# Batch 0 of an FFT-mixing and gated-FFN kernel: slices of x folded as they land, another order of sums, products and weight preparation

## The chip, the cores and the metric

The kernel runs on one core of a Trainium2 chip. The core has a matrix engine (TensorE, PE in the profile; its weight loads are PEld), three engines for elementwise work (VectorE or DVE, ScalarE or ACT, GpSimd or POOL), a queue engine that issues most transfers (SyncE or SP), and 16 DMA engines. The metric is the device time in microseconds.

## The reference

```python
# x: (8, 3008, 256) float32; w_gate, w_val: (256, 1536); w_out: (1536, 256)
X = np.fft.fft(x, axis=1)
X = np.fft.fft(X, axis=2)
x = X.real.astype(np.float32).reshape(8 * 3008, 256)
gate = 1.0 / (1.0 + np.exp(-(x @ w_gate)))
val = x @ w_val
out = (gate * val @ w_out).astype(np.float32)
```

The three weights are float64, because a float32 array is multiplied there by a float64 scalar. The kernel is handed their bits and makes float32 of them itself.

## The kernel before, in words

The real part of the two-dimensional transform splits into sums over the sequence and sums over the 256 features. The feature sums are linear, so the kernel multiplies them into the weights once: a **merge** multiplies 256 columns of `w_gate` or `w_val` by a cosine and sine table (`dt`) and leaves them as `G1` (cosine part) and `G2` (sine part). Per batch there remain the sequence sums. x is **folded** first (rows s and S-s, s and M+s are added or subtracted, and features d and 256-d likewise), then multiplied by a cosine table (giving **P**) and a sine table (giving **Q**); the one feature without a partner, number 128, gives a single row **E**, the same for all features. The tables lie in `ST`: 126 rows, 6 slots q, 753 columns for each of cosine and sine. Each sum makes half of the rows in an even and an odd part (`ev`, `od`); `places` adds and subtracts these into `pk` (P) or `qk` (Q), two VectorE instructions a group (L504, L507) after a ScalarE copy of `ev` (L499).

The main loop then goes over 576 **steps** i: 8 batches, 6 chunks of 252 rows, 12 tiles of 128 hidden features. Three steps make a group p. A step does, in the order of the code:

- `front_a(i)`: two TensorE products of `G1` with P. In batch 0's first chunk, steps 0 to 4 (`N1 = 5`) also get E by two products of `G2` with `e0`, a tile of zeros with E in its first row.
- `part(i)`: ScalarE copies the bank, doubled, as `ae` (L611); in steps 5 to 11 VectorE adds E instead, by two instructions (L614).
- `gate_a(i-1)`: a sigmoid of the step before (ScalarE, L630), and the values of the mirrored rows, z (VectorE, L635 or L632).
- `seed(i+1)`: from step 12 on, ScalarE writes E times its weight `ge` into the next step's bank (two instructions, L595), so that the products are added to it.
- `gate_b(i-1)`: a product (L647), a sigmoid of z (L648), a second product (L649), which frees the bank; then 13 GpSimd sums per group (L653) for the last product.
- what is in `pre` and `use`: weight preparation; a part of `forms`, which makes sums of `w_out` blocks (GpSimd for g = 0, otherwise VectorE, and four ScalarE copies).
- `back`: from step 5, ten instructions a step of the output product, a block scheme with 15 products, in banks `po0` to `po4`.
- `front_b(i)`: two products of `G2` with Q, added to the same bank.
- `side`: x of later batches, tables, E rows of later chunks.

Five of the eight PSUM banks are the `po` banks. Three (`psx`) are shared by the steps' banks `pf`, merges (`ps`) without a bank of their own, and the sequence sums.

A weight (256 rows or columns of one matrix, 18 `jobs`) is loaded by `weight_load` (L288), taken apart by two ScalarE instructions (`weight_parts`, L295 and L296), put together by three VectorE instructions and one GpSimd addition (`weight_join`, L305, L306, L308, L310), and merged by `weight_use` (eight TensorE instructions, ScalarE copies L331 and L332, and two small transfers `ge` on SP, L334). Weights 0 to 9 (`KEEP = 10`) have places of their own, later ones use x's.

Every engine, SP too, works in the order in which the code issues instructions (`manual_schedule`). SP's start is: weights 0 and 1, x of batch 0 in two halves (L150), the cosine table in two halves (L192), weights 2 to 4, half the sine table, weights 5 and 6, the other half, weights 7 to 9. The sums of batch 0 wait for the folds of three slots at a time; P and E sums (24 wide matmuls, E as 128 equal rows) come before the Q sums (12). All TensorE instructions have line L134, that of the helper `mm`.

Of the kernel before, what the change touches and what calls it, by code (L numbers as in the profile page):

```python
# [81 lines left out]
def kernel(  # L82
# [61 lines left out]
    def load_x(b):  # L144
        X[b] = xp.tile([P, 4, NQ, D], F32, name="x4", tag="x4")
        for h in range(0, 4, 2):
            if b:
                nc.sync.dma_start(out=X[b][:, h : h + 2], in_=XR[b][:, h : h + 2])
            else:
                nc.sync.dma_start(out=X[b][0:NP, h : h + 2], in_=xf[b, :, h : h + 2])  # L150
# [29 lines left out]
    G1 = const.tile([P, 2, F], F32, name="G1")  # L180
    G2 = const.tile([P, 2, F], F32, name="G2")
# [8 lines left out]
    def load_table(t, nq):  # L190
        for q in range(0, NQ, nq):
            yield nc.sync.dma_start(out=ST[0][0:NP, t, q : q + nq], in_=stab[:, t, q : q + nq])  # L192
# [14 lines left out]
    def table_odd():  # L207
# [21 lines left out]
        def tangent():  # L229
# [8 lines left out]
    jobs = [(0, 0), (1, 0), (0, 1), (1, 1), (2, 0), (0, 2), (1, 2), (2, 1), (0, 3), (1, 3), (0, 4), (2, 2),  # L238
            (1, 4), (0, 5), (1, 5), (2, 3), (2, 4), (2, 5)]
    RAW, WS = {}, {}  # L240
    shared = {}
    KEEP = 10

    def weight_load(j):
# [13 lines left out]
        def home(j):  # L258

            if j in (0, 1, 2, 3, 5):  # L260
                if j > 2:
                    ws = some(5, pqp, "qk")[:, (j // 5) * 2 * WC : (j // 5 + 1) * 2 * WC]
                    return sp.tile([P, 4 * WC], F32, name="raw", tag="sf"), ws
                t = hp.tile([P, 6 * WC], F32, name="raw", tag="h")
                return t[:, 0 : 4 * WC], t[:, 4 * WC :]
            if j in (4, 6, 9):
                t = wf[:, {4: 1, 6: 2, 9: 3}[j]].rearrange("p m n -> p (m n)")
                return t[:, 0 : 4 * WC], t[:, 4 * WC : 6 * WC]
            t = some(10, cp, "c")
            if j == 7:  # L270
                raw = pqp.tile([P, 4 * WC], F32, name="raw", tag="pk")
                return raw, t[:, 6 * WC : 8 * WC]
            return t[:, 0 : 4 * WC], t[:, 4 * WC : 6 * WC]
# [50 lines left out]
    def merge(ws, g, c, other):  # L324
# [6 lines left out]
        nc.scalar.copy(G2[:, g, cs], ps[:, WC : 2 * WC])  # L331
        nc.scalar.copy(G1[:, g, cs], ps[:, 0:WC])  # L332
# [48 lines left out]
    def fold_ops(b, nq):  # L381
# [51 lines left out]
        else:  # L433

            def half1(q):
                point(nc.vector, 2, 3, q)
                first(nc.vector, 2, 3, q)
                for blk in range(2):
                    across(nc.vector, blk, q)
                    feat(nc.vector, *parts[blk], q)  # L440

            def half2(q):
                across(nc.vector, 0, q)
                feat(nc.vector, *parts[0], q)
                across(pool, 1, q)
                feat(pool, *parts[1], q)
            for q in qs:
                point(nc.vector, 0, 1, q)
            first(nc.vector, 0, 1, slice(0, NQ))
            point(pool, 2, 3, qs[1])  # L450
            first(pool, 2, 3, qs[1])
            ops += [lambda: half1(qs[0]), lambda: half2(qs[1])]
        for blk, (v, r) in enumerate(parts):
            if b and blk:
                W[b, blk] = v[:, :, HD:D], r[:, :, HD:D]
                continue
            W[b, blk] = (v[:, :, 0:HD], r[:, :, 0:HD],
                         v[:, :, HD : HD + 1].to_broadcast([v.shape[0], NQ, P]))
# [56 lines left out]
    def seq_start(b):  # L515
        PQE[b] = [pqp.tile([P, NK + 1], F32, name=name, tag=name) for name in ("pk", "qk")]
        if not b:
            PQE[b].append(op.tile([P, NK + 1], F32, name="ek", tag="os"))
# [5 lines left out]


# [60 lines left out]
    N1 = 5  # L586

    def seed(i):
# [5 lines left out]
        for g in range(2 if i >= NFT else 0):  # L594
            nc.scalar.activation(PF[i][:, g], EK[i // NFT], AF.Copy, scale=ge[:, g, f : f + 1])  # L595

    def front_a(i):
        (pk, *_), ks, _, _, fs = cut(i)
        if i < NFT:
            seed(i)  # L600
        for g in range(2):
            mm(PF[i][:, g], G1[:, g, fs], pk[:, ks], i < NFT and g == 0, True)
        for g in range(2 if i < N1 else 0):
            mm(PF[i][:, g], G2[:, g, fs], shared["qk"][:, 4 * WC : 4 * WC + CH], False, True)

    def part(i):
# [3 lines left out]
        if not N1 <= i < NFT:  # L610
            nc.scalar.activation(AP[i], PF[i], AF.Copy, scale=2.0)  # L611
            return
        for g in range(2):
            nc.vector.scalar_tensor_tensor(out=AP[i][:, g], in0=pqe[2][:, ks],  # L614
                                           scalar=ge[:, g, f : f + 1], in1=PF[i][:, g],
                                           op0=ALU.mult, op1=ALU.add)
# [6 lines left out]
    def gate_a(i):  # L623
# [7 lines left out]
        if N1 <= i < NFT:  # L631
            nc.vector.scalar_tensor_tensor(out=z[:, :, ::-1], in0=AP.pop(i), scalar=2.0, in1=PF[i],  # L632
                                           op0=ALU.mult, op1=ALU.subtract)
        else:
            nc.vector.tensor_tensor(z[:, :, ::-1], AP.pop(i), PF[i], op=ALU.subtract)  # L635
# [6 lines left out]
    def gate_b(i):  # L642
# [5 lines left out]
        nc.scalar.activation(pf[:, 0], z[:, 0], AF.Sigmoid)  # L648
        nc.vector.tensor_tensor(h[:, fh, n:], pf[:, 0], z[:, 1], op=ALU.mult)  # L649
# [94 lines left out]

    nc.gpsimd.memset(nil, 0.0)
# [3 lines left out]
    for j in range(2):  # L749
        weight_load(j)  # L750
    load_x(0)
    for _ in load_table(0, NQ // 2):
        pass
    for j in range(2, 5):
        weight_load(j)
    sines = load_table(1, NQ // 2)
    next(sines)
    for j in range(5, 7):
        weight_load(j)
    next(sines)  # L760
    for j in range(7, KEEP):
        weight_load(j)

    def weight_round(*js):
        for j in js:
            weight_parts(j)
            weight_join(j)

    weight_parts(0)
    weight_parts(1)  # L770
    weight_join(0)
    weight_join(1)
    weight_use(0)
    weight_use(1)
    seq_start(0)

    e0 = shared["qk"][:, 4 * WC : 4 * WC + CH]
    nc.gpsimd.memset(e0, 0.0)
    other = {(0, 0): (4, None), (0, 1): (4, None), (0, 2): (0, 1), (1, 2): (2, 3)}
    cos = [seq_group(0, blk, what, other.get((blk, what))) for blk in range(2) for what in (0, 2)]  # L780
    for i, f in enumerate(fold_ops(0, NQ // 2)):
        f()
        for sums, _, _ in cos:
            sums(*range(i * NQ // 2, (i + 1) * NQ // 2))
    sin = [seq_group(0, blk, 1, other.get((blk, 1))) for blk in range(2)]
    for i in range(2):
        for sums, _, _ in sin:
            sums(*range(i * NQ // 2, (i + 1) * NQ // 2))
    evacuate = [then for _, then, _ in cos + sin]
    for then, js in zip(evacuate, ((2, 3), (4,), (5,), (6,), (7,), (8,))):  # L790
        weight_round(*js)
        then()()
    nc.scalar.dma_start(out=ed[0:1], in_=PQE[0][2][0:1])
    nc.vector.tensor_copy(e0[0:1], PQE[0][2][0:1, 0:CH])
    weight_parts(9)
    for j in range(KEEP, KEEP + 3):
        weight_load(j)
    weight_use(2)
# [8 lines left out]
    pre, use = {}, {}  # L807
    for j, i in enumerate((0, 1, 2, 3, 4, 5, 6, 7, 9), 9):
        if i:
            pre.setdefault(i - 1, []).append(lambda j=j: weight_parts(j))  # L810
        pre.setdefault(i, []).insert(0, lambda j=j: weight_join(j))
        if KEEP <= j < len(jobs) - 3:
            at(i, lambda j=j: weight_load(j + 3))
    for j, i in enumerate((0, 0, 1, 2, 0, 3, 4, 5, 4, 6, 7, 8, 8, 8, 11), 3):
        use.setdefault(i, []).append(lambda j=j: weight_use(j))
# [123 lines left out]
```

## Time and profile before

| | |
|---|---|
| time, median of 3 runs | 1955.66 us (1949.49 to 1955.82) |
| profiled execution: span (no other time of it is given) | 1953.1 us |
| busy: PE, PEld | 1915.7 us (98%), 1788.2 us (92%) |
| busy: DVE, ACT, POOL | 1457.9 us (75%), 1332.5 us (68%), 1598.4 us (82%) |
| granted TensorE clock, mean | 0.995 |
| first Q product of step 0 starts at | 58.12 us |
| step 15 starts at | 122.31 us |

A row of the timeline gives start, duration, engine, line, operation, what is written and read, the number of instructions, and in brackets the idle time ahead of it with what ended it. A row of the windows gives the stretch, its length, the busy time (and count) of PE, PEld, DVE, ACT and POOL, the granted TensorE clock, the share of the DMA engines and GB/s. A TensorE matmul of 32-bit numbers shows as two instructions.

### The profile page before, as it was taken

Reading aid. Unit: us, or ns where it says so; the run is one execution under the profiler, and the core shown is the slowest. Engines: PE = TensorE matmul, PEld = TensorE weight load, DVE = VectorE, ACT = ScalarE, POOL = GpSimd, SP = SyncE. Lnnn points to the kernel's source line nnn. Section 1 sums busy time; section 2 is a strip of 40 time slices with the busy share of each in tenths; the row PEclk is TensorE's granted clock in tenths of the full one; section 3 lists DMA queues with packets and bytes.
Section 4 is the critical chain, followed back from the end, with each engine's and each line's share of the span. In section 5 each row is a group of like instructions: output and inputs, shape, how many; then the busy total and the mean of one; then the engine's idle time right before and its main releaser. Section 6 shows DMA issues by size and latency. Waiting matters only on the chain.

```text
span 1953.1 us, 34554 instructions
## 1 busy us (share of the span) xinstructions
PE 1915.7 (98%) x11252; PEld 1788.2 (92%) x11252; DVE 1457.9 (75%) x3271; ACT 1332.5 (68%) x3122; POOL 1598.4 (82%) x2853
## 2 busy tenths in 40 slices
PE   6999999999999999999999999999999999999997
PEld 3789889999999999999999999999999999999997
DVE  5877787787777877777777777777777777777776
ACT  2567757776777677776777767777677766777775
POOL 3679998997889788997889869888789886777776
PEclk8999999999999999999999999999999999999999
DMA  9352513112012020212012021111200110011011
GB/s 268 91 134 20 117 32 111 46 25 82 14 46 58 16 79 14 60 46 79 14 25 80 16 79 25 45 51 21 83 17 14 22 20 14 14 22 20 14 20 27
DMA packets 169746, 96.78 MB, mean 50 GB/s; under 512 B 133858, under 2 KB 161636, under 8 KB 167020
## 3 DMA queue, kind: packets, MB, share of 16 engines
q1 hardware_dynamic: 167610, 94.06, 20.2%
q8 instruction: 90, 1.47, 0.3%
q10 hardware_dynamic: 1926, 0.52, 0.1%
q14 instruction: 88, 0.72, 0.1%
q0 software_dynamic: 32, 0.00, 0.0%
HBM read 69.83 MB, written 46.71 MB: 60 GB/s over the span
## 4 chain that ended last, share of the span: by engine, by line
PE 92%; DVE 4%; DMA 2%; ACT 1%; issue 0%; SPq 0%; POOL 0%; DVEq 0%; ACTq 0%; POOLq 0%
PE pf L134 48%; PE po L134 40%; PE ev L134 3%; DMA st<-in_stab_dram 1%; DVE c L700 1%; PE od L134 1%; DMA ge<-G 1%; PE ps L134 1%; DVE z L635 0%; ACT pf L648 0%; DVE h L649 0%; DVE h L647 0%; DVE ae L614 0%; DVE wf L370 0%; DMA raw<-in_moe_w_gate_dram 0%
## 5 line engine op out<-in xcount | busy, mean ns | idle before, releaser
L653 POOL TENSOR_TENSOR sf<-h 128x168 f32<-128x168 f32 (+1 forms) x960 | 533.3, 575 | 222.3 <-DVE h L649 222.3
L653 POOL TENSOR_TENSOR sf<-h,sf 128x168 f32<-128x168 f32 (+1 forms) x1152 | 645.1, 580 | 63.0 <-DVE h L649 62.6
L134 PE MATMUL pf<-qk,G 128*128 128x252 f32 (+1 forms) x2304 | 583.1, 376 | 4.3 <-DVE ae L614 2.4
L134 PE MATMUL pf<-pk,G 128*128 128x252 f32 (+1 forms) x2304 | 583.2, 376 | 1.5 <-DVE h L649 1.5
L649 DVE TENSOR_TENSOR h<-pf,z 128x252 f32<-128x252 f32 (+1 forms) x576 | 241.7, 420 | 425.0 <-ACT pf L648 425.0
L595 ACT ACTIVATE pf<-ek,ge 128x252 f32<-128x252 f32 (+1 forms) x1128 | 531.6, 471 | 18.6 <-DVE h L649 0.2
L134 PE MATMUL po<-sf,wf 128*128 128x168 f32 (+1 forms) x3072 | 529.9, 305 | 0.0
L611 ACT ACTIVATE ae<-pf 128x504 f32<-128x504 f32 (+1 forms) x569 | 335.5, 590 | 233.3 <-PE pf L134 232.3
L134 PEld LDWEIGHTS pf<-pk,G 128*128 128x128 f32 x2304 | 436.1, 190 | 55.3 <-DVE h L649 2.6
L134 PEld LDWEIGHTS po<-sf,wf 128*128 128x128 f32 x3072 | 472.7, 190 | 8.2
L134 PE MATMUL po<-h,wf 128*128 128x168 f32 (+1 forms) x2688 | 476.0, 305 | 0.2 <-DVE wf L367 0.2
L700 DVE TENSOR_TENSOR c<-c 128x168 f32<-128x168 f32 (+1 forms) x949 | 447.7, 504 | 5.5 <-ACT c L677 0.2
L134 PEld LDWEIGHTS po<-h,wf 128*128 128x128 f32 x2688 | 427.5, 190 | 17.2 <-DVE wf L367 0.6
L134 PEld LDWEIGHTS pf<-qk,G 128*128 128x128 f32 x2304 | 409.8, 190 | 31.9 <-ACT ae L611 3.2
L635 DVE TENSOR_TENSOR z<-ae,pf 128x504 f32<-128x504 f32 (+1 forms) x569 | 378.7, 666 | 23.4 <-ACT h L630 21.8
L630 ACT ACTIVATE h<-pf 128x252 f32<-128x252 f32 (+1 forms) x576 | 218.1, 379 | 156.3 <-PE pf L134 151.9
L648 ACT ACTIVATE pf<-z 128x252 f32<-128x252 f32 (+1 forms) x576 | 214.4, 372 | 114.8 <-DVE h L647 112.2
L647 DVE TENSOR_TENSOR h<-h,pf 128x252 f32<-128x252 f32 (+1 forms) x576 | 232.7, 404 | 0.0
L653 POOL TENSOR_TENSOR sf<-sf 128x168 f32<-128x168 f32 (+1 forms) x192 | 111.0, 578 | 15.1
L653 POOL TENSOR_TENSOR sf<-sf,h 128x168 f32<-128x168 f32 (+1 forms) x192 | 105.2, 548 | 0.0
L677 ACT COPY c<-po 128x504 f32<-128x504 f32 (+1 forms) x144 | 81.9, 569 | 2.6 <-PE po L134 2.6
L134 PE MATMUL ev<-st,x 63*128 63x189 f32 (+3 forms) x372 | 73.6, 348 | 10.2 <-DVE x L398 7.9
(138 smaller groups left out, 874.9 us busy)
## 6 DMA issues: line engine op xcount, KB each, us to landing
x<-xr SPq DMA_DIRECT2D x14, 1536.0 KB
out_dram<-os SPq DMA_DIRECT2D x380, 56.0 KB
xr<-in_xf_dram SPq DMA_DIRECT2D x14, 768.0 KB
xr<-in_xf_dram SPq DMA_DIRECT2D x35, 256.0 KB
ek<-ed SPq DMA_DIRECT2D x39, 126.0 KB
out_dram<-os SPq DMA_DIRECT2D x288, 7.0 KB
st<-in_stab_dram SPq DMA_DIRECT2D x4, 1111.9 KB
x<-in_xf_dram SPq DMA_DIRECT2D x2, 1512.0 KB
```

The lines of the kernel that those rows point to most:

```text
L134: nc.tensor.matmul(o, l, r, start=start, stop=stop, skip_group_check=True)
L595: nc.scalar.activation(PF[i][:, g], EK[i // NFT], AF.Copy, scale=ge[:, g, f : f + 1])
L611: nc.scalar.activation(AP[i], PF[i], AF.Copy, scale=2.0)
L630: nc.scalar.activation(H[p][:, fh, 0:n], PF[i][:, 0], AF.Sigmoid)
L635: nc.vector.tensor_tensor(z[:, :, ::-1], AP.pop(i), PF[i], op=ALU.subtract)
L647: nc.vector.tensor_tensor(h[:, fh, 0:n], h[:, fh, 0:n], pf[:, 1], op=ALU.mult)
L648: nc.scalar.activation(pf[:, 0], z[:, 0], AF.Sigmoid)
L649: nc.vector.tensor_tensor(h[:, fh, n:], pf[:, 0], z[:, 1], op=ALU.mult)
L653: nc.gpsimd.tensor_tensor(block(p, dst), block(p, a), block(p, b), op=(ALU.subtract, ALU.add)[op])
L677: (nc.vector.tensor_copy if t == 1 or t == 3 and not last else nc.scalar.copy)(C[0][:, 3 * t * R : 3 * (t + 1) * R], PO[t][:, 0 : 3 * R])
L700: engine.tensor_tensor(t[:, dst * R : (dst + 1) * R], *v, op=(ALU.subtract, ALU.add)[op])
```

## The change

x of batch 0 comes in three transfers of two slots each, 128 rows high, its tables in slices of the same two slots, each as 112 and 14 rows. VectorE folds a slice as it lands (`third`, `feats`), and GpSimd no longer takes part. E is summed as four rows, each in its own 32-column tile of TensorE, and put into `e0` and a row `er` by small instructions. 18 matmuls of zeros (`warm`) are issued ahead of the first merges and sums. Weights 2 and 3 are merged between the slices. The P products of steps 0 to 2 go between slices of the Q sums. The order of the weights is another, so is the moment of each preparation, and `weight_join` stands between the two products of `gate_b`. `N1` is 3: E is added by TensorE in steps 0 to 2 and by ScalarE's seeds from step 3. A merge copies its bank by one ScalarE instruction in place of two.

```diff
+    def load_third(j):
+        q = slice(2 * j, 2 * j + 2)
+        rows = xf.rearrange("b p h q d -> (b p) h q d")
+        nc.sync.dma_start(out=X[0][:, :, q], in_=rows[0:P, :, q])
...
-    def load_table(t, nq):
-        for q in range(0, NQ, nq):
-            yield nc.sync.dma_start(out=ST[0][0:NP, t, q : q + nq], in_=stab[:, t, q : q + nq])
+    def load_table(t, j):
+        q = slice(2 * j, 2 * j + 2)
+        for rows in (slice(0, 112), slice(112, NP)):
+            nc.sync.dma_start(out=ST[0][rows, t, q], in_=stab[rows, t, q])
...
-    jobs = [(0, 0), (1, 0), (0, 1), (1, 1), (2, 0), (0, 2), (1, 2), (2, 1), (0, 3), (1, 3), (0, 4), (2, 2),
-            (1, 4), (0, 5), (1, 5), (2, 3), (2, 4), (2, 5)]
+    jobs = [(0, 0), (1, 0), (0, 1), (1, 1), (0, 2), (1, 2), (2, 0), (2, 1), (0, 3), (1, 3), (0, 4), (1, 4),
+            (2, 2), (0, 5), (1, 5), (2, 3), (2, 4), (2, 5)]
...
-    KEEP = 10
+    KEEP = 12
...
-        nc.scalar.copy(G2[:, g, cs], ps[:, WC : 2 * WC])
-        nc.scalar.copy(G1[:, g, cs], ps[:, 0:WC])
+        nc.scalar.copy(G[:, :, g, cs], ps.rearrange("p (h n) -> p h n", h=2))
...
+            def third(q):
+                a, m = x4[:, 0:3:2, q], x4[:, 1:4:2, q]
+                tt(a[:, :, :, 1:D], a[:, :, :, 1:D], m[:, :, :, D - 1 : 0 : -1], op=ALU.add)
+                tt(a[:, :, :, 0], a[:, :, :, 0], m[:, :, :, 0], op=ALU.add)
+                across(nc.vector, 0, q)
+                across(nc.vector, 1, q)
+
+            def feats(q):
+                v, r = x4[:, 0:2, q], x4[:, 2:4, q]
+                nc.vector.memset(r[:, :, :, 0:1], 0.0)
+                lo, hi = v[:, :, :, 1:HD], v[:, :, :, D - 1 : HD : -1]
+                tt(r[:, :, :, 1:HD], lo, hi, op=ALU.subtract)
+                tt(lo, lo, hi, op=ALU.add)
...
+    def e0_sums(j):
+        if not j:
+            E0["ps"] = bank("pe", NB - 1)
+        for q in (2 * j, 2 * j + 1):
+            for blk in range(2):
+                c0, n = ((0, NE), (NE, NO))[blk]
+                row = (2 * blk + q % 2) * TB
+                mm(E0["ps"][row : row + 1, 0:n], W[0, blk][2][:, q], ST[0][0:NP, 0, q, c0 : c0 + n],
+                   not j, j == N3 - 1)
+
+    def e0_row():
+        ...   # three ScalarE copies of rows of the bank, two VectorE sums into e0[0:1]
+
+    def e0_rest():
+        ...   # places(er, 0, ...), places(er, 1, ...), then er to ed[0:1] by SP
...
-    N1 = 5
+    N1 = 3
...
-        for g in range(2 if i >= NFT else 0):
+        for g in range(2 if i >= N1 else 0):
             nc.scalar.activation(PF[i][:, g], EK[i // NFT], AF.Copy, scale=ge[:, g, f : f + 1])
...
-        if not N1 <= i < NFT:
-            nc.scalar.activation(AP[i], PF[i], AF.Copy, scale=2.0)
-            return
-        for g in range(2):
-            nc.vector.scalar_tensor_tensor(out=AP[i][:, g], in0=pqe[2][:, ks],
-                                           scalar=ge[:, g, f : f + 1], in1=PF[i][:, g],
-                                           op0=ALU.mult, op1=ALU.add)
+        nc.scalar.activation(AP[i], PF[i], AF.Copy, scale=2.0)
...
         nc.scalar.activation(pf[:, 0], z[:, 0], AF.Sigmoid)
+        for f in between:
+            f()
         nc.vector.tensor_tensor(h[:, fh, n:], pf[:, 0], z[:, 1], op=ALU.mult)
...
+    for f, *a in ((weight_load, 0), (weight_load, 1), (load_third, 0), (load_table, 0, 0), (weight_load, 2),
+                  (load_third, 1), (load_table, 0, 1), (weight_load, 3), (load_third, 2), (load_table, 0, 2),
+                  (load_table, 1, 0), (weight_load, 4), (load_table, 1, 1)):
+        f(*a)
...
+    warm(12)
...      # weights 0 and 1: parts, join, merge
+    warm(6)
+    for j in range(N3):
+        folds[2 * j]()
+        e0_sums(j)
+        folds[2 * j + 1]()
+        for sums, _, _ in cos:
+            sums(2 * j, 2 * j + 1)
+        if j < 2:
+            weight_round(2 + j)
+    weight_load(5)
+    load_table(1, 2)
+    for j in range(6, 9):
+        weight_load(j)
+    put = [then() for _, then, _ in cos]
+    e0_row()
+    for f in put:
+        f()
...      # EK[0] from e0's row, by way of DRAM
+    for j in range(N3):
+        for sums, _, _ in sin:
+            sums(2 * j, 2 * j + 1)
+        front_a(j)
+        if j < 2:
+            weight_parts(4 + j)
+            weight_join(4 + j)
+    for _, then, _ in sin:
         then()()
+    weight_use(4, 0)
+    weight_parts(6)
+    for j in range(9, KEEP + 3):
         weight_load(j)
...
-    for j, i in enumerate((0, 1, 2, 3, 4, 5, 6, 7, 9), 9):
+    for j, i in ((6, 0), (7, 1), (8, 2), (9, 3), (12, 4), (10, 4), (11, 5), (13, 6), (14, 7), (15, 7), (16, 8),
+                 (17, 10)):
         if i:
             pre.setdefault(i - 1, []).append(lambda j=j: weight_parts(j))
-        pre.setdefault(i, []).insert(0, lambda j=j: weight_join(j))
+        mid.setdefault(i, []).append(lambda j=j: weight_join(j))
...
-    for j, i in enumerate((0, 0, 1, 2, 0, 3, 4, 5, 4, 6, 7, 8, 8, 8, 11), 3):
-        use.setdefault(i, []).append(lambda j=j: weight_use(j))
+    for j, i, other in ((5, 0, 1), (6, 0, None), (7, 1, None), (8, 3, 2), (9, 4, 3), (12, 4, None), (10, 5, None),
+                        (11, 6, None), (13, 7, None), (14, 8, None), (15, 8, None), (16, 8, None), (17, 10, None)):
+        use.setdefault(i, []).append(lambda j=j, other=other: weight_use(j, other))
+    at(1, e0_rest)
...
     for i in range(count):
-        front_a(i)
-        if N1 <= i < NFT:
-            part(i)
+        if i >= N3:
+            front_a(i)
         if i:
             gate_a(i - 1)
-        if not N1 <= i < NFT:
-            part(i)
-        if i0 <= i + 1 < count:
+        part(i)
+        if N1 <= i + 1 < count:
             seed(i + 1)
         if i:
-            gate_b(i - 1)
+            gate_b(i - 1, mid.pop(i, []))
```

The number behind a weight in `use` is a `po` bank for its merge; `None` means one of the three `psx` banks, or for `w_out` that nothing is merged. (`parts` of weights in the last lists are issued one step ahead.)

## The prediction

> **What bounds the kernel now.** I read the page first: span, slices, chain.
>
> ```profile
> span 1953.1 us, 34554 instructions
> ...
> PE   6999999999999999999999999999999999999997
> ...
> PEclk8999999999999999999999999999999999999999
> ...
> PE 92%; DVE 4%; DMA 2%; ACT 1%; issue 0%; SPq 0%; POOL 0%; DVEq 0%; ACTq 0%; POOLq 0%
> ```
>
> TensorE fills every slice but the first (a slice is 48.8 us) and the last. What changes batch 0's opening can only move the moment from which TensorE runs without a break. Next, the windows, cut at the stages of the TensorE timeline:
>
> ```profile
> 45.00:54.60 9.60, 7.30 (x20) 4.74 (x21) 5.85 (x12) 4.45 (x8) 3.13 (x3) 0.82 0.33 108
> 54.60:76.10 21.50, 21.50 (x102) 18.94 (x101) 14.52 (x28) 13.89 (x35) 16.54 (x23) 1.00 0.41 121
> 76.10:100.10 24.00, 21.06 (x105) 17.36 (x104) 21.68 (x43) 10.46 (x29) 17.20 (x23) 1.00 0.27 72
> 100.10:122.30 22.20, 19.66 (x109) 17.72 (x108) 18.40 (x41) 11.41 (x34) 15.73 (x26) 1.00 0.40 131
> 122.30:153.60 31.30, 31.30 (x182) 29.49 (x181) 22.47 (x53) 22.61 (x53) 24.07 (x45) 1.00 0.71 118
> ```
>
> After the span come PE, PEld, DVE, ACT, POOL, clock, DMA. The rows are: last sine sums; steps 0 to 4; steps 5 to 8; steps 9 to 14; ten steps from 15. Steps 0 to 4 are TensorE's own (4.3 us each), steps 5 to 8 are VectorE's (21.68 busy of 24.00), and from step 15 a step takes 3.13 us, all TensorE. So I forecast the start of step 15, 122.31 us now. The TensorE timeline shows that and the waits ahead of it:
>
> ```profile
> 47.30 0.90 PE L134 MATMUL ev<-st,x 126*128 126x377 f32 x2 [2.34 <-DMA st<-in_stab_dram]
> ...
> 83.32 1.12 PE L134 MATMUL pf<-pk,G 128*128 128x252 f32 x4 [0.73 <-DVE h L649]
> ...
> 122.31 1.01 PE L134 MATMUL pf<-pk,G 128*128 128x252 f32 x4
> ```
>
> First it waits for the sine table's last half, later for `gate_b` to give a bank back.
>
> Unit prices from the timelines: a merge 1.73, P or Q products of a step 0.85, back 1.43, a wide sequence matmul 0.636 (1.27 a pair); conversion of a weight: ScalarE 1.15, VectorE 1.5 alone and up to 2.8 beside GpSimd, GpSimd 1.3.
>
> **The change, part by part.**
>
> *Opening.* Ahead of the last cosine slice the queue now holds 0.26 MB of `dtab`, four weights of 0.52, three x slices of 1.05, three table slices of 0.76: 7.7 MB, where before only weights 0 and 1 stood ahead of x and the cosines. At the 271 GB/s of 0 to 45 us, first bytes at 2 us, x is there at 27.8 and the table at 30.6. A slice's fold is worked out from rows of other widths: 1020 elements 1.2 (765 take 0.96), four times 510 at 0.65, small ones 0.2, so 4.0, 2.6 of it before the E sums. The E sums in column tiles cost little: later in this trace twelve such matmuls take 2.1:
>
> ```profile
> 203.86 2.09 PE L134 MATMUL pe<-st,x 126*7 126x377 f32 x24
> ```
>
> Four are 0.7, against 2.5 for wide ones. Last slice: fold to 31.8, P sums 2.5, so the cosines end near 34, not at 45 (31 at 302 GB/s, 35 at 262, the ends of the ten-us windows with a full queue). The 18 warm-up matmuls lie ahead of weight 0 (TensorE idles to 8.79 now) and ahead of the first fold: nothing on the path; uncovered, 2.5 for the last six. The merges of weights 2 and 3 fit between slices.
>
> *To Q of step 0.* ScalarE copies one ev and three rows (1.9), VectorE two short sums and four of 0.54 (2.5): P of step 0 starts at 38.3, the first sine slice lying in that wait. Then P, sines, P, sines, P in turn: 0.85+0.85 with E, 2.5, 1.7, 2.5, 1.7, to 48.5 (the last sine slice has landed: 11 MB, 43). Merges 4 and 5 to 52.0. ScalarE has G of 4, parts of 6 and `part(0)` in its queue; Q of step 0 starts at 52.5, not at 58.12, with two more merges and P of two more steps done (6.9 of TensorE).
>
> *Steps 0 to 4.* Now conversions 6 to 9 lie here, three behind the kernel before, and `mid` puts each between the two products of `gate_b`. VectorE after ScalarE gets to the first sigmoid (54.5): z and h 0.95, join 7 1.5, h 0.4, the row's four E sums of 0.54, z and h 0.95, join 8 2.0, that is to 62.5. Behind it GpSimd has, in order, add 8 (1.3), seven sums of 0.56, two forms sums of 0.73, add 9 (1.3): 70.5. Merge 9 waits for that and step 4 ends near 73.1 (now 76.08). Weight 9 was joined four steps ahead of its merge; now it is one. The doubled E products of steps 3 and 4 (1.7) and VectorE's E form from step 5 (0.85 a step) go; neither is what is late here.
>
> *Steps 5 to 8.* ScalarE now seeds the next step's bank before the second half of `gate_b`. With three `psx` banks, two steps and the seed hold all, so merges 10, 11, 13 and 14 must wait for the last product of `gate_b`; before they took the former merge's bank. Steady steps show that wait:
>
> ```profile
> 125.64 0.38 ACT L630 ACTIVATE h<-pf 128x252 f32<-128x252 f32 x1
> ...
> 126.49 0.59 ACT L611 ACTIVATE ae<-pf 128x504 f32<-128x504 f32 x1 [0.47 <-PE pf L134]
> ...
> 126.97 0.97 ACT L595 ACTIVATE pf<-ek,ge 128x252 f32<-128x252 f32 x2
> ...
> 128.28 0.42 DVE L649 TENSOR_TENSOR h<-pf,z 128x252 f32<-128x252 f32 x1 [1.20 <-ACT pf L648]
> ```
>
> Q of the step before ends at 125.60 and the bank is free at 128.70: 3.1 us, hidden in a steady step. Here merge, back and Q (4.0) stand behind it in TensorE's queue. With a join of 1.5 in the gap it is 3.4, with two (step 7) 5.2: steps 6, 7, 8 take 7.4, 9.2, 7.4. Step 5 is worse: GpSimd has six sums, two forms sums and add 12 left (76.6), ScalarE's four forms copies wait for add 12 (77.4), its sigmoid, copy, seeds and sigmoid and VectorE's join and product follow (80.8), then 4.0: 84.8. Step 8 ends at 108.8, where before it was 100.10. The floor is 3.4 plus 4.0 a step, the ceiling joins of 2.8 each (5 us more in all).
>
> *Steps 9 to 14.* VectorE is relieved: 6 steps of 3.13 and 0.5 for join 17, 19.3 instead of 22.2. Step 15 starts at 128.1: 5.8 late.
>
> *The clock.* Idle time can cost more than itself:
>
> ```profile
> 45.30:48.70 3.40, 1.40 (x5) 0.90 (x6) 0.38 (x1) 0.10 (x1) 0.88 (x1) 1.00 0.68 249
> 48.70:52.10 3.40, 3.40 (x7) 1.95 (x6) 2.74 (x6) 3.21 (x7) 1.06 (x1) 0.50 0.05 19
> ...
> 103.30:106.80 3.50, 2.38 (x15) 2.03 (x13) 3.28 (x6) 0.51 (x2) 2.78 (x5) 1.00 0.72 240
> ```
>
> A 3.4 us stretch with 1.40 busy was followed by one at clock 0.50 (1.7 us lost); one with 2.38 busy was not. After the change TensorE idles some 6.9 in step 5 and 2.5, 4.3, 2.5 in steps 6 to 8. From 0 to 6.8 us; I take 1.7, the longest gap, as the others depend on how they lie to the stretches. The Trainium skill's page "TensorE: Matmul & The Clock Gate" (section "Why this matters for your kernels") warns of idle gaps over some 3 us, which speaks against this change: by it two gaps count, 1.7 us more than my sum; the trace's gap of 2.34 us shows that shorter ones can do it.
>
> Sum: 5.8 + 1.7 = 7.5 late, on the span 1953.1. The profile gives no time around it; the median of the runs, 1955.66, lies 2.6 above. So 1955.66 + 7.5, **1963**. A measurement of this kernel can tell about 0.5%, 9.8 us, from no change.
>
> **The rivals.** *Faster: the lead of the opening survives.* If GpSimd's adds aren't queued behind its sums and the merges aren't held, step 4 ends with VectorE's joins near 69, steps 5 to 8 take the 24.0 of today, and step 15 starts at 112.3: 1945.7. With nothing but TensorE's work from 48.5 (eight merges, 13.8; three Q, 2.5; twelve steps of 1.7; ten backs) it would be 99.6: 1933. For it: TensorE's 6.9 us already done, and VectorE without the E form. Against it: the banks, which I read off the order of the code. 0.15.
>
> *Slower beyond the bound: the clock halves after every gap.* It decides in steps 5 to 8 as soon as a 3.4 us stretch has under about 2 us of TensorE work; four times 1.7 in place of one: 1968; with the slower joins 1973. For it: the 48.70 row. Against it: no halving after the waits of 76 to 110 us. 0.28.
>
> *The change doesn't bring its slices early.* Pieces down to 84 KB and two short rows per table slice could land as late as the two halves do; then the cosines end at 45 again and the 11 us come on top: 1974. For it: only four transfers of the queue are in flight around 12 to 23 us, and each next one is issued as an earlier one lands. Against it: the 271 GB/s hold through that. 0.05.
>
> **How the numbers follow.** The forecast has the remaining 0.52; its own range is 1953 to 1967 (joins at 1.5 or 2.2, cosines at 31 or 35, clock 0 or 3.4). Nearly all of it lies within 0.5%, 1945.9 to 1965.4. Faster: 0.15, the first rival. Slower: 0.28 and 0.05 and 0.02 of the forecast's upper end, 0.35. Same: 0.50. The 8-in-10 range reaches into both sides, 1945 to 1971, and leaves out the faster half of the first rival and the tops of the others.
>
> **What would show it.** Opening: last P sum before 38, P of step 0 before step 1's Q, no wait on the sine table. Steps 3 to 5: TensorE waiting on GpSimd's L310-line add, ScalarE's copies too. Steps 5 to 8: each merge released by `gate_b`'s last product, steps of over 7 us. Clock: a 0.50 stretch after step 5. Wrong would be: merges of steps 5 to 8 that start right behind P; step 15 before 115; or another difference beyond step 15, where I expect 3.13 us a step as now.

## The result, and the profile after

| | before | changed |
|---|---|---|
| time, median | 1954.01 us (1949.49 to 1955.82) | 1973.1 us (1971.96 to 1974.29) |
| profiled execution: span, time | 1953.1, not given | 1970.1, 1971.96 |
| first Q product of step 0 | 58.12 | 52.92 |
| step 15 starts | 122.31 | 139.65 |

The changed kernel is slower, by a ratio of 1.0105 [1.0089, 1.0122]. The forecast of 1963 had the sign right and less than half of the size; the range, to 1971, ends below the result.

The page of the changed kernel, span, slices and chain:

```profile
span 1970.1 us, 34616 instructions
...
PE   8689999999999999999999999999999999999997
...
PEclk9799999999999999999999999999999999999999
...
PE 92%; DVE 3%; ACT 1%; issue 0%; POOL 0%; DVEq 0%; ACTq 0%
```

The first digit of PE went from 6 to 8: the opening is fuller, as meant. But the second and third (a slice of this longer span is 49.3 us) are now 6 and 8 where before only nines stood, and the clock's second digit is 7. From there on the rows are those of before. The windows, cut at the starts of P of steps 5 to 9 and 15 (columns as before: PE, PEld, DVE, ACT, POOL, clock, DMA share, GB/s):

```profile
52.90:73.60 20.70, 13.85 (x44) 10.15 (x45) 16.61 (x31) 16.42 (x37) 15.31 (x19) 0.75 0.47 160
73.60:88.60 15.00, 6.89 (x28) 5.65 (x28) 8.52 (x15) 4.64 (x12) 10.53 (x15) 0.77 0.11 36
88.60:98.00 9.40, 6.79 (x28) 5.83 (x27) 5.14 (x9) 4.97 (x10) 4.48 (x7) 0.82 0.02 0
98.00:111.20 13.20, 8.10 (x28) 6.88 (x27) 5.21 (x9) 3.85 (x8) 2.64 (x2) 0.74 0.16 43
111.20:118.90 7.70, 5.09 (x28) 4.39 (x27) 4.18 (x8) 3.50 (x10) 4.46 (x7) 1.00 0.18 65
118.90:139.65 20.75, 18.97 (x110) 17.64 (x108) 17.03 (x34) 14.96 (x37) 13.93 (x24) 1.00 0.43 139
139.65:170.95 31.30, 31.30 (x182) 29.50 (x181) 22.39 (x53) 22.59 (x53) 24.04 (x45) 1.00 0.71 120
```

Steps 5, 6 and 7 (rows two to four) took 15.0, 9.4 and 13.2 us, and no engine is busy for as much as three quarters of them: these are waits on one another, at a lowered clock. Ten steps from 15 take the same 31.30 as before, so everything lies ahead of 139.65: step 15 starts 17.3 us later, the span is 17.0 longer. The timeline of TensorE shows how:

```profile
36.57 0.90 PE L134 MATMUL od<-st,x 126*128 126x377 f32 x2 [2.22 <-DVE pk L507]
...
38.58 1.01 PE L134 MATMUL pf<-pk,G 128*128 128x252 f32 x4
...
52.92 1.12 PE L134 MATMUL pf<-qk,G 128*128 128x252 f32 x4 [0.55 <-ACT ae L644]
...
70.95 1.99 PE L134 MATMUL ps<-wf,dt 128*128 128x256 f32 x8 [2.37 <-POOL wf L314]
...
82.75 3.71 PE L134 MATMUL ps<-wf,dt 128*128 128x256 f32 x8 [8.11 <-DVE h L675]
...
92.19 2.85 PE L134 MATMUL ps<-wc,dt 128*128 128x256 f32 x8 [2.61 <-DVE h L675]
...
104.06 3.75 PE L134 MATMUL ps<-wx,dt 128*128 128x256 f32 x8 [5.10 <-DVE h L675]
...
114.78 1.97 PE L134 MATMUL ps<-wx,dt 128*128 128x256 f32 x8 [2.61 <-DVE h L675]
...
128.75 0.84 PE L134 MATMUL po<-h,wf 128*128 128x168 f32 x4 [1.78 <-DVE wf L370]
```

No row waits for a table any more. The merges of steps 5 to 8 all wait for L675, `gate_b`'s last product, 18.4 us together. And three of the four run long: 3.71, 2.85, 3.75 where 1.97 is the price at full clock.

### The profile page after: what moved, and what is told of

Its sections match the earlier page's. It is cut to its first block, busy times and chain, and to the rows that moved or that the text cites. A ratio compares the mean times of both kernels' runs of the same rounds, so it can differ in the third digit from the quotient of the medians.

```text
span 1970.1 us, 34616 instructions
## 1 busy us (share of the span) xinstructions
PE 1921.9 (98%) x11280; PEld 1792.9 (91%) x11280; DVE 1460.2 (74%) x3262; ACT 1343.6 (68%) x3136; POOL 1589.3 (81%) x2847
## 4 chain that ended last, share of the span: by engine, by line
PE 92%; DVE 3%; ACT 1%; issue 0%; POOL 0%; DVEq 0%; ACTq 0%
PE pf L134 48%; PE po L134 40%; PE ev L134 2%; DVE c L726 1%; PE ps L134 1%; DVE z L659 1%; PE od L134 1%; DVE h L675 0%; DVE h L671 0%; ACT pf L672 0%; DVE wx L312 0%; DVE wx L310 0%; DVE wf L370 0%; DVE os L736 0%; PE pe L134 0%
## 5 line engine op out<-in xcount | busy, mean ns | idle before, releaser
L629 ACT ACTIVATE pf<-ek,ge 128x252 f32<-128x252 f32 (+1 forms) x1146 | 539.9, 471 | 18.9
L675 DVE TENSOR_TENSOR h<-pf,z 128x252 f32<-128x252 f32 (+1 forms) x576 | 241.4, 419 | 415.2 <-ACT pf L672 415.2
L659 DVE TENSOR_TENSOR z<-ae,pf 128x504 f32<-128x504 f32 (+1 forms) x576 | 383.1, 665 | 43.5 <-ACT h L658 41.9
L736 DVE STREAM_TRANSPOSE os<-c 128x256 f32<-128x256 f32 x192 | 73.6, 421 | 0.4 <-issue 0.3
```

What stands on the lines that cost most here:

```text
L736: nc.vector.transpose(os_[0][:, s, 0:nb, h, :], t[:, c0 : c0 + nb * TB])
```

## The experiments

The experiments ran in four groups, with the kernel before beside each: medians 1950.87, 1951.67, 1951.12 and 1951.05, single runs up to 1958.5. Ratios are to the kernel before of the same group.

### 1. The seed behind the merge

```diff
-        if N1 <= i + 1 < count:
+        late = 5 <= i <= 8
+        if N1 <= i + 1 < count and not late:
             seed(i + 1)
...      # gate_b, preparation, merges
+        if late:
+            seed(i + 1)
```

> The changed kernel, but in steps 5 to 8 ScalarE writes E into the next bank only after the step's merge has been issued. So the merge takes the bank that lies free and no longer waits for the second product of gate_b. Nothing else is moved. My theory (merges 10, 11, 13, 14 are held by the bank, and the idle time then halves the clock): each of these merges starts within 0.3 us of the step's P products, steps 6 to 8 take 4.9 to 6.3 us in place of 9.4, 13.2 and 7.7, step 15 starts near 120 instead of 139.65, and the time is 1953 to 1958. Rival, the preparation comes too late whatever the banks do (conversions 6 to 12 lie in the steps and VectorE, ScalarE and GpSimd pass them on): steps 5 to 8 stay within 3 us of what they took together (45), time 1970 or more.

Measured: 1957.77 (1956.46 to 1958.95), ratio to before 1.0031 [1.0019, 1.0042]; step 15 at 124.47, 15.2 us sooner than in the changed kernel. Its TensorE timeline:

```profile
79.04 3.58 PE L134 MATMUL ps<-wf,dt 128*128 128x256 f32 x8 [4.42 <-POOL wf L314]
...
84.83 1.01 PE L134 MATMUL pf<-pk,G 128*128 128x252 f32 x4
85.68 1.89 PE L134 MATMUL ps<-wc,dt 128*128 128x256 f32 x8
...
97.87 1.12 PE L134 MATMUL pf<-pk,G 128*128 128x252 f32 x4 [2.11 <-ACT pf L629]
```

The merge of step 6 now starts right behind P (85.68), 3 us before `gate_b`'s last product of that step ends (88.75); so do those of steps 7 and 8. That of step 5 waits for GpSimd instead, and the price of the late seed is on P of the next step (2.11). A bank is what the merges of steps 6 to 8 waited for, and holding it cost 15 of the 17 us between the two profiles, with the clock that those waits cost. Step 15 near 120 was expected: the wait of step 5 and the seeds ahead of P were not in that.

### 2. The gaps filled

Products of zeros are put into TensorE's gaps: into a `po` bank in steps 1, 2, 4 and 5, added to the step's own bank in steps 6 to 8. Nothing else changes.

```diff
+    def fill(n, i=None):
+        ps = bank("warm", NB - 1)[:, 0:CH] if i is None else PF[i][:, 0]
+        for _ in range(n):
+            mm(ps, zz, PQE[0][0][:, 0:CH], i is None, True)
...
+        if 6 <= i <= 8:
+            fill({6: 4, 7: 9, 8: 4}[i], i)
```

> The changed kernel, with matmuls by a tile of zeros put into TensorE's gaps of steps 1, 2 and 4 to 8 (2, 6, 5, 17, 4, 9, 4 of them); they add zeros or write a bank that nobody reads. No wait is taken away. My theory (the halved clock costs some 6.6 us in steps 5 to 7: merge, back and Q took 5.8, 5.8 and 7.1 there, where 4.0 is the price at full clock): the clock stays at 1.00 after 66 us, these take 4.0 to 4.3 each, time 1965 to 1968. Rival, the waits alone make the loss and the clock only shows it: within 2 us of 1973.

Measured: 1968.32 (1968.27 to 1970.2), ratio 1.0084 [1.0062, 1.0106], 4.8 below the changed kernel and just above the 1965 to 1968 expected. Windows from the merge to the end of Q in steps 5 and 7:

```profile
87.27:91.34 4.07, 4.07 (x22) 3.78 (x23) 1.90 (x2) 0.58 (x1) 4.07 (x7) 1.00 0.02 2
...
105.16:109.23 4.07, 4.07 (x22) 3.78 (x23) 0.00 (x0) 0.59 (x1) 0.93 (x1) 1.00 0.01 0
```

Merge, back and Q take 4.07 at clock 1.00, in all four steps. In the changed kernel the same stretch takes 5.83 (82.75 to 88.58), 5.76, 7.10 and 4.08. So the clock cost 1.76 + 1.69 + 3.03 = 6.5 us there. The whole way from P of step 5 to step 15 says the same: 59.6 us (78.11 to 137.73), where the changed kernel takes 66.0. The gain in time is smaller than that: in the profiled execution Q of step 0 started 1.7 us later than in the changed kernel, and P of step 5 at 78.11 instead of 73.63, in part behind the fills of steps 1 to 4.

### 3. The joins behind gate_b

```diff
-            gate_b(i - 1, mid.pop(i, []))
+            gate_b(i - 1)
```

The joins of that step then follow as a group.

> The changed kernel, but weight_join is issued behind gate_b and not between its two products. My theory (the bank comes back 3.1 us after Q in the best case, joins add 0.5 in steps 6 and 8 and 3 in step 7, and less idle time means less of the half clock): 1966 to 1971. Rival, the joins inside gate_b are the main cause: steps 5 to 8 near 6 us each, time 1958 or less. If the joins outside come too late for their merges: 1973 or more, with TensorE waiting on GpSimd's addition.

Measured: 1969.72 (1969.24 to 1970.08), ratio 1.0091 [1.0072, 1.011]. Its merges of steps 6, 7 and 8:

```profile
95.94 1.97 PE L134 MATMUL ps<-wc,dt 128*128 128x256 f32 x8 [2.40 <-DVE h L675]
...
103.43 1.97 PE L134 MATMUL ps<-wx,dt 128*128 128x256 f32 x8 [2.40 <-DVE h L675]
...
110.92 2.95 PE L134 MATMUL ps<-wx,dt 128*128 128x256 f32 x8 [2.40 <-DVE h L675]
```

The joins account for 0.2 us of the wait in steps 6 and 8 and for 2.7 in step 7, which has two (5.10 to 2.40). The 2.40 that stay are there with no join: ScalarE's copy and seeds ahead of the second sigmoid, and the product behind it. The third of three equal gaps, not the first two, was followed by a lowered clock (2.95). The time is within what was expected.

### 4. E by VectorE up to step 11

Seeds only from step 12, VectorE's two instructions of the kernel before in steps 3 to 11.

```diff
-        for g in range(2 if i >= N1 else 0):
+        for g in range(2 if i >= NFT else 0):
             nc.scalar.activation(PF[i][:, g], EK[i // NFT], AF.Copy, scale=ge[:, g, f : f + 1])
...
+            nc.vector.scalar_tensor_tensor(out=AP[i][:, g], in0=EK[0], scalar=ge[:, g, f : f + 1],
+                                           in1=PF[i][:, g], op0=ALU.mult, op1=ALU.add)
```

> The changed kernel, but E is added by VectorE in steps 3 to 11 as the kernel before did from step 5 (two more VectorE instructions a step, operand the broadcast row of E; no ScalarE copy, no seeds before step 12). Opening, weight order and joins stay as changed. My theory (the seeds take the third bank): merges of steps 5 to 8 are not held by gate_b, steps 5 to 8 take 24 to 28 us together, step 15 starts at 117 to 122, time 1949 to 1956. Rival, VectorE was the bound of these steps in the kernel before, so that giving it E back costs 0.85 us a step on top: 1973 or more.

Measured: 1961.46 (1959.46 to 1962.92), ratio 1.0049 [1.0033, 1.0064]: between the 1949 to 1956 expected and the rival's 1973. The merges of steps 6 to 8 start right behind P, as the bank theory says, and that of step 5 waits 4.49 us for GpSimd's addition. But P of step 8 then waits for `gate_b`'s last product (L684 there), and the clock falls behind that wait:

```profile
100.11 1.12 PE L134 MATMUL pf<-pk,G 128*128 128x252 f32 x4 [3.19 <-DVE h L684]
101.07 3.17 PE L134 MATMUL ps<-wx,dt 128*128 128x256 f32 x8
```

So the seeds are the dear way to add E in steps 3 to 8, by 11.6 us in the medians, but taking them away does not bring the opening's lead back by itself.

### 5. The seeds alone, in the kernel before

```diff
-        for g in range(2 if i >= NFT else 0):
-            nc.scalar.activation(PF[i][:, g], EK[i // NFT], AF.Copy, scale=ge[:, g, f : f + 1])
+        row = EK[i // NFT] if i >= NFT else PQE[0][2][:, 0:n]
+        for g in range(2 if i >= N1 else 0):
+            nc.scalar.activation(PF[i][:, g], row, AF.Copy, scale=ge[:, g, f : f + 1])
```

> The kernel before, with one part of the change alone: E by ScalarE's seeds from step 5 (the kernel before has VectorE add E in steps 5 to 11). Theory, that a seed ahead of the second half of gate_b takes the bank that a merge needs: the merges of steps 5 to 8 wait for gate_b's last product, 2.4 to 5 us each, TensorE's gaps lower the clock after one or two of them, and step 15 starts 5 to 12 us later than 122.3, so 1956 to 1963 where the kernel before has 1951. Rival, that steps 5 to 8 are VectorE's (21.68 busy of 24.00) and the seeds take 0.85 us a step from it: step 15 starts up to 5 us sooner, 1946 to 1951.

Measured: 1961.94 (1959.62 to 1962.7), ratio 1.0045 [1.0028, 1.0062]. Two of the five merges that wait 2.40 us each:

```profile
78.69 3.44 PE L134 MATMUL ps<-wx,dt 128*128 128x256 f32 x8 [2.40 <-DVE h L640]
...
104.52 1.96 PE L134 MATMUL ps<-wx,dt 128*128 128x256 f32 x8 [2.40 <-DVE h L640]
```

Step 15 starts at 129.24. This one part costs 10 us in a kernel without the new opening. What relieving VectorE, the rival, gives back is less than that: steps 9 to 14 take 20.64 us, where the profile of experiment 12 has 23.30, but the five steps ahead of them take 41.92 in place of 28.29.

### 6. E by TensorE to step 8, in the changed kernel

```diff
-    N1 = 3
+    N1 = 9
```

> The changed kernel with that edit alone: E by TensorE's products in steps 0 to 8, seeds from step 9. Theory, that the seed ahead of the second half of gate_b holds the bank: merges 10, 11, 13 and 14 start right behind P or wait for GpSimd's addition alone, step 15 starts at 124 to 129 instead of 139.65, the time is 1957 to 1963. Rival, that gate_b itself, with a join between its halves, is what TensorE waits for in steps 5 to 8, whoever adds E: the four waits stay, or move to Q and back, and the products come on top: 1973 to 1979.

Measured: 1960.0 (1958.51 to 1960.65), ratio 1.0045 [1.0031, 1.0059]; step 15 at 127.71, both as the theory had them. Six more pairs of products are on TensorE, and three of the four waits for L675 go (the merge of step 5 waits 3.65 us for GpSimd's addition instead). The one that stays is telling:

```profile
87.92 1.89 PE L134 MATMUL ps<-wc,dt 128*128 128x256 f32 x8
...
93.62 1.89 PE L134 MATMUL ps<-wx,dt 128*128 128x256 f32 x8
...
102.83 1.97 PE L134 MATMUL ps<-wx,dt 128*128 128x256 f32 x8 [2.40 <-DVE h L675]
```

The merges of steps 6 and 7 start at once; that of step 8, the one step in which a seed (for step 9) still stands ahead of `gate_b`, waits 2.40. It is the seed that holds the bank, not `gate_b` and its join.

### 7. The warm-up products

Experiment 1 without its 18 products of zeros.

```diff
-    warm(12)
...
-    warm(6)
```

> The late-seed kernel without the 18 warm-up products of zeros. Theory, that they lie beside waits for transfers and change nothing that the later stages see: time within 1 us of the late-seed kernel's 1957.8. Rival, that they hold the granted clock through the opening: without them the first merges and cosine sums run at half clock, the cosines end 1 to 3 us later than 34.4, and the time is 1 to 4 us up.

Measured: 1958.71 (1957.35 to 1960.42), ratio 1.003 [1.0019, 1.0041]. The first two merges take 5.37 us together, where they take 1.99 each behind the warm-up, but the cosines end at 33.46 and Q of step 0 starts at 52.67, against 33.45 and 52.65 in experiment 1. They lie beside the transfers and change nothing later that these times resolve: the kernel without them lies 7.0 us above the kernel before of its group, experiment 1 6.9.

### 8. The preparation sooner

Experiment 1 with weights 6 and 7 joined ahead of step 0, weight 7 used in step 0 instead of 1, and the others sooner.

```diff
+    for j in (6, 7):
+        weight_parts(j)
+        weight_join(j)
     weight_use(4, 0)
-    weight_parts(6)
+    weight_parts(8)
...
+    for j, i in ((8, 0), (9, 1), (10, 2), (12, 3), (11, 4), (13, 5), (14, 6), (15, 7), (16, 8), (17, 10)):
```

> The changed kernel with the seeds of steps 6 to 9 behind the merges, and with the weights 6, 7 and 8 taken apart (6 and 7 joined too) ahead of step 0, the later ones a step or two sooner. Theory, that what is left of the lateness in the late-seed kernel (step 15 at 124.47, merges 9 and 10 waiting 2.4 and 4.4 us for GpSimd's additions 9 and 12) is the order of the preparation: both waits go, step 15 starts between 115 and 119 us, the time is 6 to 9 us below the late-seed kernel's 1957.8, so 1949 to 1952. Rival, that the elementwise engines are simply full in steps 0 to 5 (VectorE and GpSimd have the same sums to do in any order): the waits move to the first sigmoids and to the start of Q of step 0, step 15 stays within 2 us of 124.5, the time within 1956 to 1959.

Measured: 1953.91 (1953.32 to 1955.72), ratio 1.0006 [0.9996, 1.0017]; step 15 at 121.27, between the two expectations. One wait went, another came. ScalarE, then TensorE:

```profile
56.25 0.66 ACT L299 ACTIVATE wf<-wf 128x512 f32<-128x512 f32 x1 [3.61 <-DMA wf<-in_moe_w_val_dram]
```

```profile
59.54 2.05 PE L134 MATMUL pf<-qk,G 128*128 128x252 f32 x4 [5.73 <-ACT ae L644]
```

Weight 9 is not there before 56 us, and the sigmoid and copy of step 1 stand behind its conversion.

### 9. Weight 9 a step later

```diff
+    for j, i in ((8, 0), (9, 2), (10, 3), (12, 4), (11, 5), (13, 6), (14, 7), (15, 7), (16, 8), (17, 10)):
```

> The late-seed, early-preparation kernel with the order mended at one place: there ScalarE's parts of weight 9 waited 3.61 us for that weight's transfer (56.25 us) and held the first sigmoid, so that TensorE waited 5.73 for the copy of step 1 and ran its next products at half clock. Here the parts of weight 9 stand behind step 1's copy, and 10, 12, 11, 13 and 14 a step later than there. Theory, that this one wait is what is left of the lateness: the wait ahead of Q of step 1 falls to between 1 and 2 us, 3 to 7 us are won, step 15 starts between 114 and 118.5, the time is 1947 to 1951. Rival, that the elementwise engines are full in any order: the wait comes back at merges 9 and 10 on GpSimd's additions, step 15 stays within 2 us of the 121.3 there, 1952 to 1956.

Measured: 1954.07 (1952.64 to 1956.67), ratio 1.0016 [1.0007, 1.0025]; step 15 at 120.41. The wait of step 1 fell from 5.73 to 1.10 and the time did not fall: weight 12's addition, a step later now, held ScalarE's four copies for 4.94 us, and merge, Q and P around 70 to 80 us waited 1.75, 2.12 and 2.41. This went the rival's way.

### 10. The same with E by TensorE to step 8

`N1 = 9` in that kernel.

> The same, with E added by TensorE's two products in steps 0 to 8 and ScalarE's seeds from step 9 only. Theory, that the bank is what a seed costs: with no seed in steps 3 to 8 no merge waits for gate_b's last product, the products' 0.85 us in each of six steps lie in TensorE's waits for the larger part, and the 3.98 us that P of step 6 waited for its seed goes too: 2 to 5 us sooner than the kernel beside it, step 15 at 111 to 115. Rival, that TensorE becomes the bound there: six times 0.85, so up to 5 us later than the kernel beside it.

Measured: 1953.33 (1952.05 to 1954.65), ratio 1.0011 [1.0002, 1.0019]; step 15 at 121.36. No difference from the kernel beside it that these times resolve, which is neither the 2 to 5 us of the theory nor the loss of the rival. That the six pairs of products took what the seeds' waits gave would fit; no run shows the two apart.

### 11. Four places of the order mended

```diff
-    for j in range(9, KEEP + 3):
+    for j in (9, 10, 12, 11, 13, 14):
         weight_load(j)
...
+    for j, i in ((8, 0), (9, 2), (12, 3), (10, 3), (11, 4), (13, 5), (14, 6), (15, 7), (16, 8), (17, 11)):
...      # weight 17 is used in step 11 instead of 10
```

> The kernel with E on TensorE to step 8 and the early preparation, with four places of its order mended: weight 12 is loaded ahead of 11 and its join goes from step 4 to 3, so that its GpSimd addition stands ahead of the group's sums; joins 10, 11 and 13 a step sooner; join and use of weight 17 from step 10 to 11, behind the forms that step 11's back needs. Theory, that the remaining waits (VectorE 5.2 us and ScalarE 5.1 for the addition of weight 12 at 75 us; TensorE 1.88 and 1.29 behind them, 1.79 for the forms) are order alone: they go, 4 to 7 us, step 15 starts between 114 and 117.5, the time is 1946 to 1949.5, below the kernel before. Rival, that GpSimd's stream (sums 7 us a group, forms and additions) sets these steps: the sums come later by what the additions come earlier, back waits for them, and step 15 stays within 2 us of 121.4, 1952 to 1955.

Measured: 1950.84 (1948.91 to 1951.43) beside 1951.05 of the kernel before, ratio 0.9994 [0.9985, 1.0003]; step 15 at 119.14. Some 2.5 of the expected 4 to 7 us came, so the time lies between the theory's and the rival's. None of its merges of steps 4 to 8 runs at half clock, and those of steps 6 and 7 start right behind E:

```profile
75.40 1.97 PE L134 MATMUL ps<-wf,dt 128*128 128x256 f32 x8 [2.02 <-DVE h L675]
...
82.48 1.89 PE L134 MATMUL ps<-wc,dt 128*128 128x256 f32 x8
...
88.19 1.89 PE L134 MATMUL ps<-wx,dt 128*128 128x256 f32 x8
```

It equals the kernel before and does not beat it: this opening and these steps can be had at no loss, 22 us under the changed kernel. What took the opening's lead is not shown by a run; the six pairs of products by themselves are 5.1 us of TensorE.

### 12. The kernel before, once more

> The kernel before, unchanged, for a second profile of it. Its profiled execution has a span of 1953.1, while its 58 unprofiled comparison runs have a median near 1951, so a span near 1949. Theory, that the profiled execution was one of the long ones because of half-clock stretches in its opening (18.0 to 28.2 and 48.7 to 52.1 us): a profile with a span under 1950 shows one of them gone, and step 15 starts 3 to 5 us before 122.3. Rival, that the difference lies behind step 15 (a stretch late in the execution, or waits spread over it): step 15 starts within 1 us of 122.3 in a short execution too.

Measured: 1952.1 in one run, span 1950.1, step 15 at 119.46. Two rows of its TensorE timeline, against 47.30 with a wait of 2.34 and 58.12 in the first profile:

```profile
43.62 0.90 PE L134 MATMUL ev<-st,x 126*128 126x377 f32 x2 [0.18 <-DMA st<-in_stab_dram]
...
54.19 1.01 PE L134 MATMUL pf<-qk,G 128*128 128x252 f32 x4
```

The half-clock stretch from 48.7 to 52.1 is gone, that of 18.0 to 28.2 is still there (0.56). The first 18 us moved 305 GB/s instead of 277, and the wait for the sine table all but went (0.18), with the lowered clock behind it. The span narrowly misses the expected 1950, and step 15 starts 2.9 us sooner where 3 to 5 were expected; but the difference lies where the theory has it. So the profiled execution that the prediction was built on was one of the longer ones, by 3.0 us, 2.9 of them ahead of step 15. That is why two profiles differ by 17 and the medians by 22: 17.0 between the spans, these 3.0, 1.1 by which the changed kernel's median lies above its profiled execution, and 1.0 by which this second profile of before lies above the median of its group.

## Why the prediction was right or wrong

Its own milestones against the profile after:

| | predicted | measured |
|---|---|---|
| cosines end | near 34 | 33.72 |
| P of step 0 | 38.3 | 38.58 |
| products and sines end | 48.5 | 48.75 |
| Q of step 0 | 52.5 | 52.92 |
| step 4 ends | 73.1 | 73.63 |
| addition of weight 12 ends | 76.6 | 77.85 |
| merge of step 5 | 80.8 | 82.75 |
| step 5 ends | 84.8 | 88.58 |
| steps 6, 7, 8 | 7.4, 9.2, 7.4 | 9.37, 13.21, 7.70 |
| steps 9 to 14 | 19.3 | 20.79 |
| step 15 | 128.1, and 1.7 for the clock | 139.65 |

*Right: the opening.* Every moment up to the end of step 4 came within 0.6 us. The slices land in time, the E sums in column tiles take 0.81 per four, and Q of step 0 starts 5.2 us sooner than in the profile before. Of these 5.2 most belong to that one execution: the old opening's Q of step 0 starts at 54.19 in experiment 12 and at 53.00 in experiment 5. The opening's lead is the work done ahead of that moment, two merges and P of two steps, more than the moment itself.

*Right: where the lead goes.* Merge 9 waits for GpSimd, the forms' copies for the addition of weight 12 behind GpSimd's sums, and the merges of steps 5 to 8 for `gate_b`'s last product. Four rows of the changed kernel, GpSimd, ScalarE (two) and VectorE, give the chain of step 5:

```profile
76.57 1.28 POOL L314 TENSOR_TENSOR wx<-wx 128x512 int32<-128x512 int32 x1
...
77.87 0.31 ACT L377 ACTIVATE wf<-wx 128x128 f32<-128x128 f32 x1 [4.31 <-POOL wx L314]
...
79.42 0.98 ACT L629 ACTIVATE pf<-ek,ge 128x252 f32<-128x252 f32 x2
...
82.19 0.41 DVE L675 TENSOR_TENSOR h<-pf,z 128x252 f32<-128x252 f32 x1
```

Experiments 1 and 5 show the bank from both sides: taking the hold away wins 15 us here, putting it into the kernel before loses 10 there. Both numbers hold the waits and the clock behind them.

*Wrong: the term for the clock.* It was 1.7, one gap, out of a range of 0 to 6.8; experiment 2 prices it at 6.5, three of the four gaps (1.76, 1.69, 3.03, 0). The failed step is "I take 1.7, the longest gap, as the others depend on how they lie to the stretches": that the others depend on their place in the stretches is a reason to expect some of them, not none. The rival that halves after every gap, at 0.28, is what happened but for step 8. Its 6.8 for the clock is close to the 6.5 measured, in part by chance: one gap cost nothing and another nearly twice 1.7. The upper end of its price, 1973, was reached for another reason than the one it gave, four slow joins: of the 5.1 us of further waits below, one slow join is 1.0. The clock was lowered in steps 1 to 3 too (0.75 in the first row of the windows), which the prediction did not have. That this cost little is argued and was not tested by itself: GpSimd, for which the merge of step 4 waits, works without a break from 62.67 to 79.08.

*Wrong, smaller: the waits.* The milestones without the clock miss by 11.55 - 6.48 = 5.1 us. Step 5's start is 0.5 late and its bank 1.5 more (GpSimd's addition 1.3 late: the thirteen sums ahead of it took 8.95 us, and at 0.56 each the prediction had 7.28); step 7 has 1.0 (one join instruction of 1.40 beside GpSimd's work), steps 6 and 8 have 0.6; steps 9 to 14 have 1.5, where back of step 11 waits 1.78 for forms, a wait for which the sum had nothing. All have the same sign: here, where three in-order engines wait for each other, durations taken by themselves gave a floor. The two terms, 6.5 - 1.7 = 4.8 and 5.1, are the 9.85 us by which step 15 came later than the 129.8 of the sum.

*The base.* The sum started at 1955.66, the median of three runs then shown. The kernel before lies near 1951 in its later runs, so the change costs about 22 us and not the 17 that this base suggests. The absolute forecast is hardly touched by that, because the working gave moments of the changed kernel: 1963 less 129.8 leaves 1833.2 behind step 15, and the profiled execution has 1971.96 - 139.65 = 1832.3.

## What to carry to other kernels

A seed written early into a rotating bank is not free because the engine that writes it has time: ask who wants that bank in the same step, and try the write behind that user first. An opening that gets TensorE busy sooner gained nothing here, with a chain of three elementwise engines in a fixed order as the next stage; work out which addition or copy stands ahead of the first sigmoid before moving the preparation. And where a change makes several gaps on TensorE, charge the lowered clock for each of 2.77 us or more, as every one of those in these traces had it, and for about half of those from 1.9 to 2.6 us.

## What the runs showed of the hardware

*Gaps and the clock.* The fourteen traces together have 59 waits of TensorE of at least 1.9 us that end between 9 and 150 us. All 21 waits of 2.77 us and more were followed by a lowered clock (0.50 to 0.68, the mean of the 4 us behind them). Of the 38 waits of 1.90 to 2.61 us, 18 were (0.57 to 0.88), and 20 kept 1.00. So among the shorter gaps it is not the length that decides. In the changed kernel a gap of 2.61 us was followed by half clock in step 6 (a merge of 2.85) and not in step 8 (1.97); gaps of 2.40 were followed by merges of 3.44 and 1.96 in experiment 5. The Trainium skill's page "TensorE: Matmul & The Clock Gate" (section "Why this matters for your kernels") warns of gaps over some 3 us; two of the four gaps are that long, and a third cost 1.69 all the same. The same page (section "What's actually happening") says that activity is judged over stretches of about 3.4 us that run on freely; the rows agree with that, though no run here shifted a gap against such a stretch. Products of zeros do hold the clock (1.00 in experiment 2).

*VectorE and GpSimd take turns.* Three rows of the changed kernel's opening, VectorE, GpSimd, VectorE:

```profile
9.97 1.22 DVE L441 TENSOR_TENSOR x<-x 126x1020 f32<-126x1020 f32 x1
10.14 2.19 POOL L314 TENSOR_TENSOR raw<-raw 128x512 int32<-128x512 int32 x1 [1.60 <-issue]
11.11 1.24 DVE L442 TENSOR_TENSOR x<-x 126x4 f32<-126x4 f32 x1
```

GpSimd's addition, 1.28 elsewhere, shows 2.19: until VectorE's is done at 11.19, then 1.14 more, about its own time. And VectorE's sum of four elements takes 1.24, ending at 12.35 just behind GpSimd's 12.33. This happens for each of the three slices, and the fold of the first took 5.3 us (9.97 to 15.25) where the prediction had 4.0 from its widths. The join's instruction of step 7 that took 1.40 us, and takes 0.43 alone, also ran beside a GpSimd addition. The Trainium skill's page "SBUF — State Buffer" (section "Terms") has it as a pair of ports that one of the two holds for a whole instruction while the other is blocked; these rows agree.
